# Attention's last blocks, token routing and the first expert weights, in another order

## The chip, the cores and the metric

One core of a Trainium2 chip runs the whole program in one launch. The metric is the device time in microseconds (us); of the kernel before there are three timed runs. About 0.2% (1.15 us) is what a measurement of this kernel can tell from no change.

## What is computed

Three layers follow each other, on 4 sequences of 576 tokens with 8 heads of 64 (512 columns):

```python
scores = q @ k.T / 8;  ret = scores * gamma[h] ** (s - t) for s >= t, else 0;  x = ret @ v
logits = x @ w_gate;  local = sigmoid(x @ w_local)
e[s] = argmax(logits[s]) if s == 0 or local[s] < 0.5 else e[s - 1]
x[s] = softmax(logits[s])[e] * (relu(x[s] @ w1[e]) @ w2[e])          # 8 experts, 512 -> 1024 -> 512
h = relu(x @ w_in);  u, v = halves of h;  v = (v - mean) / std
out = (u * (w_spatial @ v + b_spatial)) @ w_out
```

The expert of a token can be that of the token before it, so routing needs a scan along each sequence. All of it is computed in float32 (large products as three products of split operands).

## The kernel before, in words

**Attention** works on 18 blocks of 128 tokens. Blocks 0 to 15 are chunk c = j // 4 of sequence b = j % 4; blocks 16 and 17 (the *late* blocks) each hold the last 64 tokens of two sequences. For each block there are: `scores` (16 products k by q into the PSUM tiles sc0 and sc1, multiplied on DVE by a decay table into pm, or into ST for a late block, L299), `scaled` (POOL makes qh and kt, or a part of ST, L312 to L320), `state_update` (16 products kt by v into st, added on DVE to the running state Sbd; after a sequence's fourth chunk also into MV, which the late blocks read), `outputs` (products of Sbd by qh and of v by pm into oT, copied by ACT as xT, L366; for a late block MV by ST, L353) and `rows` (products of xT with an identity beside the gate's weights into tx, L379: that turns the block and gives its logits L, which DVE reduces, L387, and ACT copies the rows to xb, L391).

**Routing** runs for each chunk of four blocks (routing 0 to 3) and for the two late blocks (routing 4). It is a generator, advanced one step at a time between the blocks' work: the best expert of each token and a mask (L411 to L439); two small products `ap` that put tokens along the row (L444), an ACT copy uaT, two DVE scans Fc (the expert carried on, and its count); `op` (L456) gives counts of other sequences, `offs` and GF the place of each token; `pp` (L475) brings the places back to the tokens, pos_i (L478); then POOL scatters the rows of x to their place in x_sorted, one indirect DMA for each block (L480). The last step updates the tables cum, D and Pk (L491 to L505).

After routing 4 the experts are ordered by their number of tokens: key, rank, RR; gidx (which rows the experts' blocks hold), permi (which expert comes when). permi is read into a register of SP for the load of the first expert weight (`load_w(0)`, L879), and POOL gathers the first expert's two blocks with gidx (L843). `tables` computes cnt (blocks beyond the capacity; all engines read it and branch, `overflow`), the expert's starts Sr and Sri, the rows for the way back yidx, and permi2, which the loads of weights 1 to 3 use. Then PE transposes the gathered blocks (L857), ACT and DVE split them (xH L858, xL L859) and the weights (wH L888, wL L889, for each 512 KB tile), and the expert's products run (L901 to L903). The weights have four staging buffers and are split two tiles ahead.

**What sets the order.** In the attention loop the order of PE's instructions is the program's; DVE, ACT, POOL and SP are ordered by the tile scheduler. Each block's loads are issued two blocks ahead into five buffers; the late blocks are loaded in the same way, in iterations 14 and 15. PSUM tiles have one buffer each (sc0, sc1, oT, st, tx), two for routing's. After routing 4 the scheduler orders all engines, up to the section with the first weights, where PE, SP, DVE and ACT follow the program. `keep_warm` puts products of zeros on PE (L202): 14 at the start, TAIL_WARM between the steps of routing 4, WARM[1] = 34 behind the tables.

The change touches `load_blk`, `views`, `scores`, `scaled`, `outputs`, `rows`, `routing`, the loop over the blocks and what follows it up to gidx, `tables`, and the place of `load_w(1)` to `load_w(3)`.

Of the kernel before, what the change touches and what calls it, by code (L numbers as in the profile page):

```python
# [20 lines left out]
D = H * DH  # L21
# [3 lines left out]
P = 128  # L25
# [6 lines left out]
WARM = (14, 34, 2, 4)  # L32
# [120 lines left out]
def fused(tc, blk, wgl, w1, w2, wv, wu, ws, wo, bs, cst, out, dbg=None, stop=9, caps=CAPS):  # L153
# [3 lines left out]
    with top:  # L157
# [19 lines left out]
        iotap = cp.tile([P, 9], F32, name="iotap")[:, :1]  # L177
# [4 lines left out]
        ctab = cp.tile([P, 5, 8], F32, name="ctab")  # L182
# [22 lines left out]
        with ExitStack() as ph1:  # L205
# [10 lines left out]
            def load_blk(j, parts=(0, 1)):  # L216
                if j not in btiles:
                    btiles[j] = bp.tile([P, BLKW], F32, name=f"blk{j}", tag="blk")
                t = btiles[j]
                for p_ in parts:  # L220
                    lo, hi = ((0, 1024), (1024, BLKW))[p_]
                    if j >= 16 and p_ == 1:
                        for hf in range(2):
                            sl = slice(hf * 64, hf * 64 + 64)
                            SP.dma_start(out=MV[j - 16][hf][sl].rearrange("p h c -> p (h c)"), in_=blk[j, sl, 1536:])
                        hi = 1536
                    SP.dma_start(out=t[:, lo:hi], in_=blk[j, :, lo:hi])

# [3 lines left out]
            MV = [[c1.tile([P, H, DH], F32, name=f"mv{i}_{hf}") for hf in range(2)] for i in range(2)]  # L232

# [17 lines left out]

            identB = c1.tile([P, P], BF16, name="identB")
            jB = c1.tile([P, 64], BF16, name="jB")

            def small_constants():
# [4 lines left out]
                V.tensor_copy(iotap, cs("iota_p"))  # L260

# [14 lines left out]
            def views(j):  # L276
                t = btiles.pop(j)
                c, b = (j // 4, j % 4) if j < 16 else (4, None)
# [26 lines left out]
            def scaled(j):  # L305
                d = blks[j]
                if j >= 16:
                    d["ST"] = [wk.tile([P, H, 64], F32, name=f"ST{hf}", tag=("qh", "ST1")[hf]) for hf in range(2)]
                    tab = cs("q4").rearrange("p (h t) -> p h t", h=H)
                    for hf in range(2):  # L310
                        sl = slice(64 - hf * 64, P - hf * 64)
                        G.tensor_tensor(d["ST"][hf][sl], d["kk"][sl], tab[sl], op=ALU.mult)  # L312
                    return
# [7 lines left out]
                d["kt"] = kt  # L321

# [46 lines left out]
            def rows(j):  # L369
                xT = blks[j]["xT"]  # L370
                if j == 17:
                    tx = [psc.tile([P, 512], F32, name=f"tx{g}", tag=("sc1", "st")[g]) for g in range(2)]
                else:
                    tx2 = pso.tile([P, 2, 512], F32, name="tx")
                    tx = [tx2[:, g] for g in range(2)]
                for pr in range(4):
# [4 lines left out]
                if j == 17:  # L381
# [4 lines left out]
                else:  # L386
                    V.tensor_reduce(L[:, j, :], tx2[:, :, :2 * TW].rearrange("p g (h c) -> p c g h", h=2)[:, P:],  # L387
                                    axis=AX.XY, op=ALU.add)
                xb = xp.tile([P, D], F32, name="xb")
# [7 lines left out]
            zero8 = c1.tile([P, 8], F32, name="zero8")  # L397
            G.memset(zero8, 0.0)
            tabs = dict(cum=[zero8], D=[])
            kio = cs("iota_pb")[:, None, :].to_broadcast([P, 8, 4])  # L400

            def routing(c):
# [7 lines left out]
                m = wk.tile([P, nb, 1], F32, name="m", tag="rm")  # L410
                V.tensor_reduce(m, Lg, axis=AX.X, op=ALU.max)  # L411
                r = wk.tile([P, nb, 1], F32, name="r", tag="rr")
                V.tensor_scalar(r, Ls[:, :, 8:9], GATE_TH, None, op0=ALU.is_lt)
                if c == 0:
                    V.tensor_scalar(r, r, cs("first"), None, op0=ALU.max)
                er = wk.tile([P, nb, 8], F32, name="er", tag="rer")
# [3 lines left out]
                nr_ = wk.tile([P, nb, 1], F32, name="nr_", tag="rnr")  # L420
                ua = wk.tile([P, 2, 4, 8], BF16, name="ua")
# [873 lines left out]
```

## Time and profile before

| what | us |
|---|---|
| median of three runs | 575.78 (575.36 to 575.84) |
| the profiled execution's own time | 577.63 |
| its span, first to last instruction | 575.9 |
| PE busy in the span | 550.9 (96%) |
| attention and routing, up to the first expert product | about 118 |

The span is counted from the first instruction; all times of rows are from there. PE's busy time says little of a single stage, so the stage that the change touches is read from the chain of waits, the timeline and the windows.

### The profile page before, as it was taken

What the parts mean: (1) busy time and instruction counts of PE and PEld (TensorE: products, weight loads), DVE (VectorE), ACT (ScalarE), POOL (GpSimd) and SP (SyncE); (2) the same over time, 40 slices, a digit from 0 to 9 for tenths busy, and PEclk for the clock granted to TensorE, in tenths of its full rate; (3) what the DMA queues carried; (4) which work ended last, traced back from release to release, by engine and by line L of the source; (5) the groups of instructions that cost most, each with busy time, mean ns of one, the idle gap of its engine ahead of it and who ended that gap; (6) DMA issues with size and microseconds to landing.
All of it is one profiled execution on the core that took longest, in us unless ns stands there. A gap on an engine that the chain in (4) does not pass through costs nothing.

```text
span 575.9 us, 11061 instructions
## 1 busy us (share of the span) xinstructions
PE 550.9 (96%) x4272; PEld 499.5 (87%) x4273; DVE 357.2 (62%) x757; ACT 221.8 (39%) x432; POOL 214.4 (37%) x174
## 2 busy tenths in 40 slices
PE   6989888899999999999999999999999899899997
PEld 3978877389999999999999998888888799689986
DVE  2779767755555769697975435997642845475510
ACT  1222223045444445455546533322433533463322
POOL 3565661635234535656445230332004346402000
PEclk9999999979999999999999999999999999899999
DMA  8987741586544474567465423445425554642012
GB/s 306 407 293 271 245 151 32 179 316 221 195 161 139 173 226 147 193 215 222 147 204 180 150 94 74 147 119 154 143 92 170 170 156 128 184 129 74 1 73 91
DMA packets 33864, 97.49 MB, mean 169 GB/s; under 512 B 5548, under 2 KB 5932, under 8 KB 33808
## 3 DMA queue, kind: packets, MB, share of 16 engines
q1 hardware_dynamic: 27504, 76.99, 40.4%
q0 software_dynamic: 5984, 19.24, 11.0%
q8 instruction: 34, 0.56, 0.4%
q10 hardware_dynamic: 320, 0.52, 0.3%
q14 instruction: 22, 0.18, 0.1%
HBM read 77.06 MB, written 18.89 MB: 167 GB/s over the span
## 4 chain that ended last, share of the span: by engine, by line
PE 80%; DVE 10%; issue 4%; DMA 3%; ACT 2%; SPq 0%; ACTq 0%; DVEq 0%
PE acc L901 12%; PE acc L902 12%; PE acc L903 12%; PE acc L1006 11%; PE acc L1007 11%; PE acc L1008 11%; PE tx L379 2%; PE sc L292 2%; DMA CS<-in_cst 2%; PE oT L363 2%; PE tp L857 1%; PE oT L359 1%; PE st L328 1%; DMA blk<-in_blk 1%; PE tp L1167 1%
## 5 line engine op out<-in xcount | busy, mean ns | idle before, releaser
L889 POOL TENSOR_TENSOR wL<-wst,wH 128x1024 fp32r<-128x1024 f32 x23 | 58.3, 2535 | 67.6 <-ACT wH L888 67.6
L889 DVE TENSOR_TENSOR wL<-wst,wH 128x1024 fp32r<-128x1024 f32 x41 | 54.3, 1324 | 43.3 <-ACT wH L888 40.6
L901 PE MATMUL acc<-xH,wH 128*128 128x256 f32 (+7 forms) x256 | 79.2, 309 | 0.2 <-issue 0.2
L902 PE MATMUL acc<-xL,wH 128*128 128x256 f32 (+7 forms) x256 | 79.1, 309 | 0.1
L902 PE MATMUL acc<-hL,wH 128*128 128x256 f32 (+7 forms) x256 | 78.3, 306 | 0.9 <-DVE hL L920 0.9
L901 PE MATMUL acc<-hH,wH 128*128 128x256 f32 (+7 forms) x256 | 78.9, 308 | 0.0
L903 PE MATMUL acc<-xH,wL 128*128 128x256 f32 (+7 forms) x256 | 78.7, 307 | 0.0
L903 PE MATMUL acc<-hH,wL 128*128 128x256 f32 (+7 forms) x256 | 77.5, 303 | 0.0
L888 ACT CAST wH<-wst 128x1024 fp32r<-128x1024 f32 x64 | 65.0, 1050 | 15.2 <-DMA wst<-in_w 14.9
L901 PEld LDWEIGHTS acc<-xH,wH 128*128 128x128 f32 x256 | 49.4, 193 | 0.8 <-ACT xH L858 0.7
L902 PEld LDWEIGHTS acc<-xL,wH 128*128 128x128 f32 x256 | 49.3, 193 | 0.4 <-DVE xL L859 0.4
L903 PEld LDWEIGHTS acc<-xH,wL 128*128 128x128 f32 x256 | 49.4, 193 | 0.1
L902 PEld LDWEIGHTS acc<-hL,wH 128*128 128x128 f32 x256 | 48.1, 188 | 1.4 <-DVE hL L920 1.4
L901 PEld LDWEIGHTS acc<-hH,wH 128*128 128x128 f32 x256 | 48.1, 188 | 0.2
L903 PEld LDWEIGHTS acc<-hH,wL 128*128 128x128 f32 x256 | 48.1, 188 | 0.1
L1006 PE MATMUL acc<-wsH,vH 128*128 128x288 f32 x128 | 38.2, 299 | 2.2 <-ACT ze L1118 1.7
L939 ACT COPY yT<-acc 128x256 f32 (+7 forms) x32 | 13.4, 418 | 68.5 <-PE acc L903 63.2
L919 ACT ACTIVATE hH<-acc 128x256 fp32r<-128x256 f32 (+7 forms) x64 | 26.7, 427 | 33.6 <-PE acc L903 32.8
L920 DVE SCALAR_TENSOR_TENSOR hL<-acc,hH 128x256 fp32r<-128x256 f32 (+7 forms) x64 | 29.6, 474 | 13.3 <-ACT hH L919 12.9
L1008 PE MATMUL acc<-wsH,vL 128*128 128x288 f32 x128 | 37.7, 295 | 0.0
L1007 PE MATMUL acc<-wsL,vH 128*128 128x288 f32 x128 | 37.7, 295 | 0.0
L1011 POOL DMA_INDIRECT vL<-z_v,yidx x18 | 18.3, 1016 | 44.7 <-DMA z_u<-ze 40.2
(229 smaller groups left out, 1286.2 us busy)
## 6 DMA issues: line engine op xcount, KB each, us to landing
wst<-in_w SPq DMA_DIRECT2D x64, 512.0 KB
blk<-in_blk SPq DMA_DIRECT2D x34, 512.0 KB
z_v<-ze SPq DMA_DIRECT2D x18, 257.0 KB
z_u<-ze SPq DMA_DIRECT2D x18, 256.0 KB
out<-ob SPq DMA_DIRECT2D x15, 256.0 KB
raw<-in_wv SPq DMA_DIRECT2D x4, 512.0 KB
raw<-in_wu SPq DMA_DIRECT2D x4, 512.0 KB
raw<-in_wo SPq DMA_DIRECT2D x4, 512.0 KB
```

Of the source, the lines that this page charges most:

```text
L888: A.copy(wH, st)
L889: (G if u % 8 in LPOOL and u > 1 else V).tensor_tensor(wL, st, wH.bitcast(F32), op=ALU.subtract)
L901: T.matmul(acc, lhsT=wH, rhs=xH, start=first, stop=False)
L902: T.matmul(acc, lhsT=wH, rhs=xL, start=False, stop=False)
L903: T.matmul(acc, lhsT=wL, rhs=xH, start=False, stop=last)
L919: A.activation(hH[:, :C], acc[:, :C], AF.Relu)
L920: V.scalar_tensor_tensor(hL[:, :C], acc[:, :C], 0.0, hH[:, :C].bitcast(F32), op0=ALU.max, op1=ALU.subtract)
L939: A.copy(yT[d // 3][:, d % 3, bass.ds(at, C)], acc[:, :C])
L1006: T.matmul(acc, lhsT=lH, rhs=rH, start=first, stop=False)
L1007: T.matmul(acc, lhsT=lH, rhs=rL, start=False, stop=False)
L1008: T.matmul(acc, lhsT=lL, rhs=rH, start=False, stop=last)
L1011: G.indirect_dma_start(out=t.bitcast(F32), out_offset=None, in_=src[:], in_offset=bass.IndirectOffsetOnAxis(ap=yidx[:, j:j + 1], axis=0))
```

## The change

- The late blocks get tiles of their own for q and k (QK) and for ST; they are loaded in iterations 6, 7, 10 and 11, POOL scales ST in place in iterations 9 to 12, and their scores are computed at the end of iterations 13 and 14, right ahead of the scores of blocks 14 and 15. The loop ends at block 15.
- Behind the loop PE, DVE and ACT follow one written order, down to gidx: outputs 16 come ahead of the turn of block 15, outputs 17 between the steps of routing 3. `rows` is cut into `turn`, `logits` and `keep`.
- Routing: the mask is computed first, and its product and the uaT copy come a step ahead of the other product; the scan reads the second operand from PSUM; offs is replaced by selx and a second product added into pp; the copies of nF and Cb go (ACT scales esum instead). The tables cum and D are written straight into ctab and dtb; their update has a step of its own, one step later.
- permi is computed ahead of gidx and of routing 4's last table update; `tables` computes cnt ahead of Sr.
- WARM[1] goes from 34 to 22; weights 1 to 3 are loaded behind the branch on cnt.

```diff
-WARM = (14, 34, 2, 4)
+WARM = (14, 22, 2, 4)
...
+            def load_late(i, part):
+                j = 16 + i
+                if part == 0:
+                    SP.dma_start(out=QK[i], in_=blk[j, :, :1024])
+                    return
+                for hf in range(2):
+                    own, oth = slice(hf * 64, hf * 64 + 64), slice(64 - hf * 64, P - hf * 64)
+                    SP.dma_start(out=MV[i][hf][own].rearrange("p h c -> p (h c)"), in_=blk[j, own, 1536:])
+                    SP.dma_start(out=ST[i][hf][oth].rearrange("p h c -> p (h c)"), in_=blk[j, oth, 1024:1536])
...
+            def scaled_late(i, hf):
+                tab = cs("q4").rearrange("p (h t) -> p h t", h=H)
+                sl = slice(64 - hf * 64, P - hf * 64)
+                G.tensor_tensor(ST[i][hf][sl], ST[i][hf][sl], tab[sl], op=ALU.mult)
...
-                oT = psc.tile([P, 4, P], F32, name="oT", tag="sc0" if j == 17 else "oT")
+                oT = psc.tile([P, 4, P], F32, name="oT", tag={16: "sc0", 17: "sc1"}.get(j, "oT"))
...
-                for kx in range(2):
+                uaT = wk.tile([32, P], F32, name="uaT")
+                for kx in (1, 0):
                     T.matmul(ap[:32, kx * P:kx * P + N], lhsT=ua[:, kx].rearrange("p b e -> p (b e)"), rhs=tm,
                              start=True, stop=True)
-                uaT = wk.tile([32, 2, P], F32, name="uaT")
-                A.copy(uaT[:, :, :N], ap[:32, :2 * P].rearrange("p (k n) -> p k n", k=2)[:, :, :N])
+                    if kx == 1:
+                        A.copy(uaT[:, :N], ap[:32, P:P + N])
+                        yield
...
+                esc = wk.tile([32, 16], F32, name="esc")
+                A.activation(esc, cs("esum", 32), AF.Copy, scale=cnt1)
...
+                selx = wk.tile([32, nb], F32, name="selx")
+                V.tensor_tensor(selx, selp, op[:32, :1].to_broadcast([32, nb]), op=ALU.mult)
+                yield
+                pp = bank("pp", "st")
+                T.matmul(pp[:, :nb], lhsT=lG, rhs=selp, start=True, stop=False)
+                T.matmul(pp[:, :nb], lhsT=lF, rhs=selx, start=False, stop=True)
+                V.tensor_scalar(pos_i[:, j0:j0 + nb], pp[:, :nb], 512.0 * c - 1.0, None, op0=ALU.add)
...
-            for j in range(NBLK):
-                if j + 2 < NBLK:
+            for j in range(16):
+                if j + 2 < 16:
                     load_blk(j + 2)
...
+                if j in (6, 7, 10, 11):
+                    load_late(j % 2, 1 - j // 10)
                 views(j)
                 scaled(j)
+                if 8 < j < 13:
+                    scaled_late((j - 9) // 2, (j - 9) % 2)
                 scores(j)
                 advance()
...
-                if j == 16:
-                    state_update(15)
+                if j in (13, 14):
+                    views(j + 3)
+                    scores(j + 3)
                 advance()
...
+            order = tc.manual_schedule(engines={ET.PE, ET.DVE, ET.Activation})
+            order.__enter__()
+            state_update(14)
+            outputs(15)
+            state_update(15)
+            rows(14)
+            outputs(16)
+            turn(15)
+            logits(15)
+            three, four = routing(3), routing(4)
+            next(three)
+            turn(16)
+            next(three)
+            keep(15)
+            next(three)
+            outputs(17)
+            next(three)
+            next(three)
+            logits(16)
+            keep(16)
+            rows(17)
+            next(four)
+            zt = psc.tile([P, 512], F32, name="zt", tag="sc0")
+            keep_warm(zt, TAIL_WARM[0])
+            next(four)
+            next(four)
+            next(three)
+            next(three, None)
+            keep_warm(zt, TAIL_WARM[1])
+            next(four)
+            keep_warm(zt, TAIL_WARM[2])
+            next(four)
+            next(four)
...
             tables()
-            for u in range(1, 4):
-                load_w(u)
...
             overflow(tot)
+            for u in range(1, 4):
+                load_w(u)
```

## Rows read from the trace of the kernel before

**Rows 1.** The page: busy time of each engine, its share of the span, instructions.

```profile
span 575.9 us, 11061 instructions
...
PE 550.9 (96%) x4272; PEld 499.5 (87%) x4273; DVE 357.2 (62%) x757; ACT 221.8 (39%) x432; POOL 214.4 (37%) x174
```

**Rows 2.** The chain of waits: start (us), duration, what.

```profile
94.00 0.21 DVE L L387
...
100.13 0.16 DVE pos_i L478
...
102.00 0.25 PE ap L444 x2
...
111.02 3.62 DMA xg<-x_sorted,gidx
...
118.42 0.58 PE acc L902
...
119.00 0.21 PE acc L903
```

**Rows 3.** Windows: length, busy PE, PEld, DVE, ACT, POOL; PEclk, DMA share, GB/s.

```profile
113.50:115.50 2.00, 0.29 (x2) 0.00 (x0) 1.19 (x1) 0.78 (x1) 1.63 (x2) 1.00 0.83 244
...
117.00:117.50 0.50, 0.48 (x3) 0.00 (x0) 0.50 (x1) 0.44 (x1) 0.50 (x1) 0.83 0.99 352
...
124.00:124.50 0.50, 0.50 (x5) 0.50 (x5) 0.50 (x2) 0.17 (x1) 0.00 (x0) 0.84 1.05 361
```

**Rows 4.** Groups of instructions, 0 to 110 us: busy us, mean ns | idle before.

```profile
L499 DVE TENSOR_TENSOR ge<-CS,cum 128x32 f32<-128x32 f32 x4 | 5.2, 1308 | 0.0
...
L501 DVE TENSOR_TENSOR Pk<-Pk,ge 128x32 f32<-128x32 f32 x4 | 0.8, 192 | 0.0
...
L312 POOL TENSOR_TENSOR ST<-blk,c_q 64x512 f32<-64x512 f32 x4 | 5.1, 1280 | 5.1 <-DMA blk<-in_blk 2.7 <-PE tx L379 2.3
```

**Rows 5.** Timeline, 67 to 95 us: start, us, engine, line [idle before].

```profile
67.66 1.16 PE L292 MATMUL sc<-blk 64*128 64x128 f32 x16
...
69.81 1.16 PE L379 MATMUL tx<-iw,xT 128*64 128x137 f32 x16 [0.38 <-ACT xT L366]
...
79.81 0.35 PE L475 MATMUL pp<-CS,GF 32*128 32x4 f32 x2 [1.24 <-DVE GF L461]
...
87.59 1.73 DVE L299 TENSOR_TENSOR ST<-sc,c_dtab 64x256 f32<-64x256 f32 x4 [0.19 <-PE st L328]
...
92.07 1.16 PE L379 MATMUL tx<-iw,xT 128*64 128x137 f32 x16
```

**Rows 6.** The chain of waits: one block's scores, a late block's outputs.

```profile
33.95 1.09 PE sc L292 x16
...
96.80 1.11 PE oT L353 x32
```

**Rows 7.** Windows of routing 3's first steps, routing 4's, and block 13 to 15.

```profile
94.20:95.45 1.25, 0.03 (x2) 0.03 (x2) 1.12 (x8) 1.14 (x3) 0.00 (x0) 1.00 0.00 0
...
100.44:101.98 1.54, 1.49 (x7) 0.60 (x7) 1.54 (x16) 0.00 (x0) 0.90 (x1) 1.00 0.00 0
...
67.66:93.23 25.57, 22.46 (x385) 20.57 (x386) 18.65 (x55) 6.24 (x16) 14.15 (x13) 1.00 0.42 136
```

**Rows 8.** Timeline, 99 to 123 us: scatters, routing 4's places, the third weight.

```profile
101.08 1.01 POOL L480 DMA_INDIRECT x_sorted<-xb,pos_i  x1 [9.76 <-DVE nr__1474 L433]
...
104.76 0.16 DVE L478 CAST pos_i<-pp 128x2 int32<-128x2 f32 x1
...
106.19 0.96 POOL L480 DMA_INDIRECT x_sorted<-xb,pos_i  x1 [0.30 <-DVE key L561]
...
122.05 1.05 ACT L888 CAST wH<-wst 128x1024 fp32r<-128x1024 f32 x1 [3.11 <-DMA wst<-in_w]
```

**Rows 9.** Timeline of SP's queue, 113 to 114 us: the second weight.

```profile
113.72 0.30 SPq L879 DMA_DIRECT2D wst<-in_w  x1
```

**Rows 10.** DMA queues, 113 to 114 us: packets, MB, share.

```profile
q0 software_dynamic: 58, 0.21, 56.6%
```

More of the change, by code (lines that the diff above doesn't have):

```diff
@@ L181, in fused @@
         Sri = cp.tile([P, 8], I32, name="Sri")
-        ctab = cp.tile([P, 5, 8], F32, name="ctab")
+        ctab = cp.tile([P, 6, 8], F32, name="ctab")
         dtb = cp.tile([P, 5, 8], F32, name="dtb")
@@ L369, in rows, with turn @@
             def rows(j):
+                turn(j)
+                logits(j)
+                keep(j)
+            def turn(j):
                 xT = blks[j]["xT"]
-                if j == 17:
-                    tx = [psc.tile([P, 512], F32, name=f"tx{g}", tag=("sc1", "st")[g]) for g in range(2)]
+                if j == 16:
+                    tx = [psc.tile([P, 512], F32, name=f"tx{g}", tag=("oT", "st")[g]) for g in range(2)]
                 else:
@@ L415, in routing @@
                     V.tensor_scalar(r, r, cs("first"), None, op0=ALU.max)
+                if not last:
+                    V.tensor_scalar(ua[:, 1], r.to_broadcast([P, 4, 8]), -1.0, 1.0, op0=ALU.mult, op1=ALU.add)
+                else:
+                    nr_ = wk.tile([P, nb, 1], F32, name="nr_", tag="rnr")
+                    V.tensor_scalar(nr_, r, -1.0, 1.0, op0=ALU.mult, op1=ALU.add)
+                    for x in range(nb):
+                        V.tensor_scalar(uv[:, 1, x], hm, nr_[:, x], None, op0=ALU.mult)
+                m = wk.tile([P, nb, 1], F32, name="m", tag="rm")
+                V.tensor_reduce(m, Lg, axis=AX.X, op=ALU.max)
                 er = wk.tile([P, nb, 8], F32, name="er", tag="rer")
@@ L440, in routing, with bank @@
                 yield
-                ap = psr.tile([P, 512], F32, name="ap", tag="rt")
+                def bank(name, tag):
+                    return psc.tile([P, 512], F32, name=name, tag=tag) if last else \
+                        psr.tile([P, 512], F32, name=name, tag="rt")
+                ap = bank("ap", "sc1")
                 tm = jB if last else identB
-                for kx in range(2):
+                uaT = wk.tile([32, P], F32, name="uaT")
+                for kx in (1, 0):
                     T.matmul(ap[:32, kx * P:kx * P + N], lhsT=ua[:, kx].rearrange("p b e -> p (b e)"), rhs=tm,
@@ L568, in fused @@
                             op=ALU.is_equal)
+            t1 = tb.tile([P, 8, 8], F32, name="t1")
+            V.tensor_tensor(t1, RR, ie[:, None, :].to_broadcast([P, 8, 8]), op=ALU.mult)
+            V.tensor_reduce(permf, t1, axis=AX.X, op=ALU.add)
+            V.tensor_copy(permi, permf)
+            next(four)
             V.tensor_scalar(Pk, Pk, float(B * S - 1), None, op0=ALU.min)
```

163 lines of the change are left out of this document (62 added, 101 removed).

## The prediction

> **What bounds the kernel now.** I first read the totals: TensorE (PE) is busy for 96% of a span of 575.9 us [rows 1], so from the first expert on the time is matmul work, and what the change can move is the time at which that work starts. The profiled execution took 577.63 us, 1.85 above the median of 575.78; sums are made on its trace, and the difference goes onto the median. Next the chain of waits from the last attention block to the first expert product [rows 2]: logits of block 15 at 94.00, places of routing 3 (L478) at 100.13, then the gather of the first expert's tokens, 3.62 us from 111.02 to its landing, and the expert product at 118.42. The reader is to see that no matmul throughput bounds this stretch: it is a chain logits, routing, scatter, gather. Last the granted clock by stretch [rows 3]: PE is nearly idle from 113.5 to 115.5, the clock falls to its lower level (1.2 GHz) within 117.0 to 117.5 and is back at 2.4 in 124.0 to 124.5. The first 6 us of expert work run at half speed, so a microsecond of delay there can cost as little as half a microsecond.
>
> **1. The loop up to block 12.** Table updates of routings 0 and 1 (L491 to L505) move one step later, behind the next block's score products, and the DVE copies into ctab and dtb, of nF and of Cb go. On the engine, nothing gets faster where PE is the bound; what can be won is PE waiting for a late DVE or ACT. L499 has a mean of 1308 ns for 32 elements a row, against 192 for L501, the same size [rows 4]; DVE falls behind, and in the second of these places tx of block 11 waits 0.38 us for xT [rows 5]. One such wait per routing, 2 x 0.38, goes: -0.75. Against it, four POOL products of 1.28 us (L312) move from blocks 16 and 17 into iterations 9 to 12 [rows 4], where POOL also issues scatters; the nearest bounds are 0 (they fit where POOL waits for blocks) and +1.28 (one stands ahead of a qh that PE wants). I take 0, since qh is made one block ahead. Loads for the late blocks stand in SP's queue at iterations 6 to 11 in place of 14 and 15; the bytes are the same, and blocks are loaded two ahead, so 0, at most +1. Step 1: -0.75, bounds -1.5 and +1.3.
>
> The Trainium skill, SBUF — State Buffer, section Who interferes with whom, says that a DVE instruction with two SBUF inputs contends with a GpSimd instruction that reads SBUF. The trace agrees: L499 has two such inputs and 1308 ns [rows 4]. By that rule alone the four POOL products would lengthen DVE's steps beside them, and the -0.75 would be nothing.
>
> **2. From scores of block 13 (67.66) to the logits of block 15.** In the kernel before, tx of block 15 starts at 92.07 and lasts 1.16, so the stretch takes 25.57 us [rows 5]; in it PE waits 1.24 for GF of routing 2 (L475) [rows 5]. The changed order has the same products for each block (scores, 16 of them, take 1.09 [rows 6]), and:
> - adds outputs of block 16, 1.11 [rows 6], now ahead of tx of block 15: +1.1.
> - puts scores 16 directly before scores 14, and 17 before 15. Both use the same two PSUM tiles, and DVE has to empty them with four products that take 1.73 in all [rows 5]. PE's queue is in order, so it waits these 1.73 less the one routing product that stands between (two ap products take 0.25 [rows 2]): 2 x 1.6 = +3.2. Behind this wait stand state, tx and outputs of the next block; nothing covers it.
> - takes away the wait for GF, as DVE and POOL carry less there: -1.2.
> - the logits of 15 no longer stand behind the ST products of block 17: they started at 94.00, 0.77 after tx ended (93.23): -0.7.
> Together +2.4. With step 1 the logits of 15 come 1.65 later, at 95.65.
>
> **3. Routing 3.** Before, 5.9 us pass from the end of these logits (94.20) to L478 at 100.13 [rows 2], because PE has tx 16, outputs 17 and tx 17 in between. New: eight DVE steps, 1.25 [rows 7], and from the ap product to the places about what routing 4 takes now, 102.00 to 104.76, 2.8 [rows 2, 8]: 4.05, with outputs 17 beside the scans. -1.9. L478 comes at 99.9, 0.25 earlier.
>
> **4. Routing 4 and the scatters.** Before, L478 of routing 4 ends at 104.92, but the first of its two scatters starts at 106.19 only: POOL issues one per 1.27 us, and the four of routing 3 begin at 101.08 [rows 8]. New: tx 17 now stands behind routing 3's pp, so its logits come some 1.2 us after 99.9, at 101.1; then eleven DVE steps 1.5 (sixteen took 1.54, some of them of routing 3 [rows 7]); then 2.55 (the 2.8 without the split uaT copy's wait); and in the fixed order routing 3's seven table steps stand before selx of routing 4. Sixteen steps in 1.54 are 0.1 each, so +0.75. Places at 105.9, end 106.05, and POOL starts about 0.8 later (100.29 to 101.08 before [rows 2, 8]): 106.85, where the queue of four, 100.85 + 5.05, is already empty. So the last two scatters, and with them the gather, come 0.65 later than before. The wait moves from POOL's queue to DVE.
>
> **5. Gather to first product.** From the last scatters to the gather and to the products nothing changes: 118.42 + 0.65. Weights 1 to 3 now wait for the branch on cnt and for permi2, which the new order of tables puts about 1 us later behind cnt. Before, SP issued the second weight at 113.72, and in the whole of 113 to 114 the gather queue alone moved bytes [rows 9, 10], the first gather landing at 114.64 [rows 2]: the weights were behind the first gather already, so taking them away saves nothing there (0; at most -0.5 for the second gather). That costs if cover goes: the third weight's cast waited 3.11 us for its DMA until 122.05 [rows 8], on an ACT that has the first hidden rows queued behind it. At half clock PE needs it only after 48 products of 0.21 us [rows 2], so 0, bounds 0 and +1.2. The warm-up products fall from 34 to 22: off the path, 0 in time; their cover for the clock is a rival below.
>
> **Sum.** +0.65 at the expert start. If the clock rises at the same place, half of it stays, +0.3; if it rises later by as much, all. I take +0.4: 576.2 on the median (578.0 on the profiled execution).
>
> **Rivals.**
> - *The bank waits are paid and nothing comes back.* Place: sc0 and sc1 between scores 16 and 14, 17 and 15. If step 1 gives 0 in place of -0.75 and the expert start carries its delay in full, 0.65 + 0.75 = +1.4: 577.2. It decides when tx of block 15 ends over 2.4 us later than 93.23. For it: DVE's 1.73 is measured and PE has nothing else to do; against: DVE loses over ten copies. 0.20.
> - *Weights late.* Place: SP behind the branch. From a second weight issued after about 115.7 (2 us late), ACT's cast holds the hidden rows and PE stops: +1.2 on top of +0.4, 577.4. 0.10.
> - *The clock.* Twelve fewer warm-up products and another place of the idle time: if the fall does not come, the 6.8 us at half speed [rows 3] are 3.4 less: 572.8; if the rise comes earlier by half of that, 574.5. Against: PE idles longer, not less. 0.12.
> - *More comes back than I count.* PE is busy for 22.5 of the 25.57 us [rows 7], so some 1.9 of waits stand there beside GF's; if 1.3 of these go too, and step 1 gives its other end (-1.5), the expert starts 1.4 earlier, 0.65 - 0.75 - 1.3: 574.4. 0.18.
> - The third part doing nothing (weights were behind the gather before) is part of my forecast.
>
> The Trainium skill, TensorE: Matmul & The Clock Gate, section What's actually happening, says that the throttled state is the default and activity releases it. The fall after the idle stretch agrees [rows 3]; by this rule fewer warm-up products make nothing better, which is why the clock rival stays small.
>
> **Numbers.** No measurable change 0.40 (own range 575.0 to 576.9; about 0.2%, 1.15 us, is what can be told from none), slower 0.30 (the first two rivals), faster 0.30 (the last two). The range leaves out the clock staying up altogether and both slow cases together: 573.4 to 578.0.
>
> **What would show it.** Right: scores 14 and 15 start about 1.7 us after scores 16 and 17 end; tx of block 15 ends near 95.6; L478's counterpart for routing 3 near 99.9 and for routing 4 near 105.9; the last scatters wait for DVE and not for POOL; second weight issued 2 us or more later without a PE wait. Wrong: scores 14 without a wait, the gather before 110.5 or after 113, a low clock over another length than 6.8 us, or a PE wait for a weight in the first expert.

## The result, and the profile of the changed kernel

The changed kernel takes 581.45 us (median of 4 runs, 581.21 to 582.34) beside 575.81 for the kernel before (4 runs, 575.36 to 577.12): a ratio of 1.0097, 95% interval 1.0078 to 1.0116. It is 5.6 us slower, outside the range of the prediction (573.4 to 578.0). Its profiled execution took 581.49, on the median; that of before lies 1.85 above its own. Ratios leave out single executions that ran over 1.5% above the fastest of their kernel; the medians in us keep them.

| | before | changed |
|---|---|---|
| span of the profiled execution | 575.9 [rows 1] | 579.7 |
| scores of block 13 start | 67.66 [rows 5] | 71.44 |
| logits of block 15 | 94.00 [rows 2] | 102.09 |
| places of routing 3 / routing 4 | 100.13 / 104.76 [rows 2, 8] | 105.94 / 112.92 |
| first gather | 111.02 [rows 2] | 118.65 |
| expert products with xL start | 118.42 [rows 2] | 126.99 |

The totals on the page of the changed kernel answer to [rows 1]:

```profile
span 579.7 us, 11039 instructions
...
PE 555.9 (96%) x4270; PEld 504.2 (87%) x4271; DVE 350.0 (60%) x736; ACT 222.9 (38%) x437; POOL 213.8 (37%) x174
```

PE is busy for 5.0 us more with two instructions fewer, so the added time is not all idleness: part of it is the same products at half the clock. Windows of the changed kernel (the columns of [rows 3], PEclk third from the end) show where:

```profile
54.00:57.00 3.00, 2.85 (x33) 2.73 (x35) 2.97 (x7) 0.06 (x1) 2.27 (x2) 0.51 0.32 105
...
88.00:91.50 3.50, 3.50 (x42) 3.48 (x43) 2.05 (x6) 0.00 (x0) 1.42 (x2) 0.52 0.05 18
...
126.20:132.20 6.00, 5.81 (x26) 5.50 (x26) 3.48 (x4) 2.49 (x4) 0.53 (x1) 0.50 1.02 372
```

Only the last of these stretches, behind the gather, exists in the kernel before ([rows 3]: 117 to 124.5, near 7 us; here it is as long). The stretches at 54 to 57 and 88 to 91.5, inside the attention loop, are new, and ahead of each of them PE had waited. A fourth stretch, 112 to 119, is new too; most of what PE does in it is warm-up products. PE's timeline from the scores of block 13 to tx of block 15 answers to [rows 5]:

```profile
71.44 1.16 PE L308 MATMUL sc<-blk 64*128 64x128 f32 x16
...
75.83 1.16 PE L308 MATMUL sc<-QK 64*128 64x128 f32 x16
...
78.15 0.46 PE L308 MATMUL sc<-blk 64*128 64x128 f32 x2 [0.99 <-PE ap L477]
...
79.08 1.13 PE L308 MATMUL sc<-blk 64*128 64x128 f32 x14 [0.48 <-DVE ST L315]
...
85.75 0.46 PE L308 MATMUL sc<-blk 64*128 64x128 f32 x2 [0.84 <-PE op L503]
...
86.69 1.13 PE L308 MATMUL sc<-blk 64*128 64x128 f32 x14 [0.48 <-DVE ST L315]
...
89.22 2.04 PE L400 MATMUL tx<-iw,xT 128*64 128x137 f32 x16
...
96.54 1.09 PE L373 MATMUL oT<-qh,Sbd 128*64 128x128 f32 x16 [1.97 <-ACT xT L380]
...
100.88 2.10 PE L400 MATMUL tx<-iw,xT 128*64 128x137 f32 x32
```

The scores of block 16 (sc<-QK) end at 76.99, those of block 14 begin at 78.15, break off and go on at 79.08, when DVE has emptied the second bank. The same comes again ahead of block 15 (85.75 and 86.69). Behind it tx takes 2.04 us, where 1.16 stands in [rows 5]. The last line holds tx of block 15 and of 16; that of 15 ends at 102.06. The stretch from 71.44 to 102.06 is 30.6 us, against 25.57 [rows 7]. As a window (the columns of [rows 7]):

```profile
71.44:102.06 30.62, 25.82 (x417) 23.77 (x418) 16.07 (x48) 6.76 (x18) 9.22 (x9) 0.94 0.20 65
```

PE is busy for 3.4 us more than in [rows 7], with the 32 products of block 16's outputs (1.1 us) and at a mean clock of 0.94 in place of 1.00, and idle for 1.7 us more.

The 3.8 us by which the scores of block 13 are late arise earlier. Timeline of POOL, DVE and PE in iterations 9 and 10:

```profile
47.67 3.99 POOL L335 TENSOR_TENSOR ST<-ST,c_q 64x512 f32<-64x512 f32 x3 [0.68 <-DMA x_sorted<-xb,pos_i]
...
50.45 1.26 DVE L452 TENSOR_TENSOR er<-CS,r 128x32 f32<-128x32 f32 x1
...
51.74 1.04 POOL L329 TENSOR_TENSOR kt<-blk,c_ktab 128x512 f32<-128x512 f32 x1
...
51.85 0.98 DVE L457 TENSOR_TENSOR w<-w,er 128x32 f32<-128x32 f32 x1
...
52.74 1.26 POOL L335 TENSOR_TENSOR ST<-ST,c_q 64x512 f32<-64x512 f32 x1
...
53.09 1.01 DVE L463 TENSOR_TENSOR ua<-CS,vr 128x32 bf16<-128x32 f32 x1
...
54.15 0.29 PE L477 MATMUL ap<-identB,ua 128*32 128x128 bf16 x1 [2.05 <-DVE ua L463]
```

Three of POOL's four moved products run back to back for 3.99 us, then a kt, then the fourth. Three DVE steps of 32 elements a row take 1.26, 0.98 and 1.01, where 0.19 is usual ([rows 4], L501): er ends with the third moved product, w with the kt, ua with the fourth. The ap product of routing 1 waits 2.05 us for ua. State update, tx and outputs stand behind it in PE's queue, and then comes the low clock of 54 to 57. The place can be told from the starts of the scores: those of block 10 come at 50.94 (51.06 in the kernel before), those of block 11 at 59.27 (55.82), and the distance stays near 3.5 to 3.8 from there on. The wait and half of the low stretch of 3.4 us are 3.75.

The chain of waits in the tail, as in [rows 2]:

```profile
102.09 0.21 DVE L L411
...
119.93 3.97 DMA xg<-x_sorted,gidx
...
126.99 0.58 PE acc L953
```

And the timeline of the steps between, DVE and POOL, as in [rows 8]:

```profile
105.94 0.16 DVE L510 TENSOR_SCALAR pos_i<-pp 128x4 int32<-128x4 f32 x1 [0.55 <-PE pp L509]
...
107.04 0.20 DVE L411 TENSOR_REDUCE L<-tx 128x9 f32<-128x36 f32 x1 [0.56 <-PE tx L400]
...
112.11 0.14 DVE L505 TENSOR_TENSOR selx<-CS,op 32x2 f32<-32x2 f32 x1
...
112.92 0.16 DVE L510 TENSOR_SCALAR pos_i<-pp 128x2 int32<-128x2 f32 x1 [0.68 <-PE pp L509]
...
113.82 1.01 POOL L512 DMA_INDIRECT x_sorted<-xb,pos_i  x1 [2.21 <-issue]
...
115.13 0.96 POOL L512 DMA_INDIRECT x_sorted<-xb,pos_i  x1 [0.30 <-issue]
...
118.65 0.98 POOL L894 DMA_INDIRECT xg<-x_sorted,gidx  x1 [2.55 <-DVE t L661]
```

From the logits of block 15 to the places of routing 3 pass 3.85 us (6.13 before). The last two scatters now wait for these places (POOL idle 2.21; the first of them starts 0.74 behind the end of pos_i, as 0.79 in the kernel before), and the gather comes 3.52 us behind the last, as before (107.45 to 111.02, 3.57). The whole expert part is then moved by the same amount: the transposes at the start of an expert, and a product of the stage behind the experts, in the changed kernel

```profile
322.91 0.80 PE L908 MATMUL tp<-identR,xg 128*128 128x128 f32 x8
...
459.12 0.40 PE L1057 MATMUL acc<-wsH,vH 128*128 128x288 f32 x1 [0.56 <-ACT ze L1169]
```

and in the kernel before, with a window behind them:

```profile
314.48 0.80 PE L857 MATMUL tp<-identR,xg 128*128 128x128 f32 x8
...
452.51 0.40 PE L1006 MATMUL acc<-wsH,vH 128*128 128x288 f32 x1 [1.73 <-ACT ze L1118]
...
496.00:500.00 4.00, 4.00 (x11) 2.78 (x10) 0.38 (x3) 1.44 (x4) 0.99 (x2) 0.57 0.60 165
```

The distance is 8.4 at the transposes. Behind the experts the kernel before waits 1.73 for ACT where the changed kernel waits 0.56, and from 496 to 500 this one execution of before ran at 0.57 of the clock, which the changed kernel's does not. These two are 2.9 of the 4.6 us by which the distance shrinks to the end; the spans differ by 3.8 us. The medians differ by 5.6, the profiled execution of before being 1.85 above its own.

### The profile page after: what moved, and what is told of

The parts are those of the page before. It is cut to its first block, busy times and chain, and to the rows that moved or that the text cites. A ratio compares the mean times of both kernels' runs of the same rounds, so it can differ in the third digit from the quotient of the medians.

```text
span 579.7 us, 11039 instructions
## 1 busy us (share of the span) xinstructions
PE 555.9 (96%) x4270; PEld 504.2 (87%) x4271; DVE 350.0 (60%) x736; ACT 222.9 (38%) x437; POOL 213.8 (37%) x174
## 3 DMA queue, kind: packets, MB, share of 16 engines
q1 hardware_dynamic: 27536, 76.99, 39.9%
## 4 chain that ended last, share of the span: by engine, by line
PE 85%; DVE 8%; issue 2%; ACT 2%; DMA 2%; SPq 0%; POOLq 0%; ACTq 0%; DVEq 0%
PE acc L952 12%; PE acc L953 12%; PE acc L954 11%; PE acc L1059 11%; PE acc L1057 11%; PE acc L1058 11%; PE sc L308 3%; PE tx L400 3%; PE oT L377 2%; PE st L342 2%; PE oT L373 1%; PE tp L908 1%; DMA blk<-in_blk 1%; PE tp L1218 1%; DMA xg<-x_sorted,gidx 1%
## 5 line engine op out<-in xcount | busy, mean ns | idle before, releaser
L318 DVE TENSOR_TENSOR pm<-sc,c_dtab 128x512 f32<-128x512 f32 x32 | 20.6, 685 | 23.3 <-PE sc L308 20.1
```

The source lines that it names most:

```text
L318: V.tensor_tensor(pm, sc[hh], tab[:, hh], op=ALU.mult)
```

## The experiments

Theory A: the waits of PE for the two score banks, and the low clock behind them. Theory B: POOL's four products in iterations 9 to 12, which hold DVE and POOL's own queue up. Theory C: the end (order of tables, weights behind the branch, 22 warm-up products). The runs were made on four chips; on three of them the kernel before takes 565 us, on one 577. Times are compared only with runs of before on the same chip, ratios with their 95% intervals.

**The scores moved within the iteration.**

```diff
                     rows(j - 2)
+                if j in (13, 14):
+                    views(j + 3)
+                    scores(j + 3)
...
                     outputs(j - 1)
-                if j in (13, 14):
-                    views(j + 3)
-                    scores(j + 3)
```

> The changed kernel (581.4 us), with the scores of blocks 16 and 17 issued between the rows and the outputs of iterations 13 and 14 (so behind state update and rows, ahead of outputs) in place of directly ahead of the scores of blocks 14 and 15. Theory A (the two waits for the score banks, near 2.0 us each, and the low clock of 87.3 to 91.9 us behind the second): the waits fall to under 0.6 each, the stretch from scores 13 to the end of tx of block 15 falls from 30.6 to about 26.5, and the time to 577 to 578. Theory B (the POOL products of iterations 9 to 12 carry the loss): the stretch falls, but scores 13 still start near 71.4, and the time stays over 579.5. Theory C (the end: order of tables, weights behind the branch, fewer warm-up products): 581.

570.32 us, before 565.35: 1.0100 [1.0071, 1.0129]. On this chip the changed kernel itself has 1.0159 (next run), so some 0.6% came back, as much as theory A expected. But the stretch from the scores of 13 to the logits of 15 is 29.9 us (63.90 to 93.79) where 26.5 was expected, against 32.3 in the next run. Timeline of DVE and PE:

```profile
67.40 3.58 DVE L439 TENSOR_SCALAR r<-L 128x4 f32<-128x4 f32 x1
...
71.25 0.23 PE L477 MATMUL ap<-identB,ua 128*32 128x128 bf16 x1 [1.63 <-DVE ua L443]
```

A DVE step of 4 elements a row took 3.58 us, and the early ap product, which needs the step behind it, waited in front of the scores of 14. The second bank wait went, the first stayed, and the clock was low from 72 to 80: part of theory A, and a first sight of theory B's mechanism.

**The products emitted later.**

```diff
-                if 8 < j < 13:
-                    scaled_late((j - 9) // 2, (j - 9) % 2)
+                if j in (14, 15):
+                    scaled_late(j - 14, 0)
+                    scaled_late(j - 14, 1)
```

> The changed kernel with POOL's four products of the late blocks moved from iterations 9 to 12 to iterations 14 and 15 (two in each, behind that block's own products). Theory B: the wait of the second ap product of routing 1 (2.05 us at 54.15) and the low clock of 54 to 57.3 go, scores 13 start near 68 in place of 71.44, and the time falls by 3 to 3.5, to 578. Theory A: 581, since what stands behind scores 13 is the loss, or slower, because the products then run beside DVE's ST products. Theory C: 581.

574.37: 1.0159 [1.0132, 1.0187]. It tested nothing: POOL's order is not written out in the loop, the products are placed where their inputs are ready, and the order of instructions on PE, DVE, ACT, POOL and SP came out as in the changed kernel. It stands here as a measurement of that kernel on this chip.

**The tables of routing 3 behind selx of routing 4.**

```diff
-            next(three)
-            next(three, None)
             keep_warm(zt, TAIL_WARM[1])
             next(four)
+            next(three)
+            next(three, None)
             keep_warm(zt, TAIL_WARM[2])
```

> The changed kernel with the table steps of routing 3 moved behind selx of routing 4. selx came at 112.11 although its product was done near 111.1. My theory of the end: places of routing 4 come 0.7 to 0.8 earlier against the logits of block 17, and so do the scatters and the gather: 580.7. If gather and expert start hang on the tables (cnt, gidx) and not on the scatters: 581.4, or up to 0.5 more.

572.17: 1.0138 [1.0102, 1.0174], not told apart from 1.0159. From the logits of block 17 to the places of routing 4 it took 6.09 (101.27 to 107.36), against 6.18 in the run before: the gain of 0.7 was not there. It appears in the pair further down (6.18 to 5.23).

**Weights and warm-up as before.**

```diff
-WARM = (14, 22, 2, 4)
+WARM = (14, 34, 2, 4)
...
             tables()
+            for u in range(1, 4):
+                load_w(u)
...
             overflow(tot)
-            for u in range(1, 4):
-                load_w(u)
```

> The changed kernel with weights 1 to 3 issued ahead of the branch again and 34 warm-up products: the third part of the change undone. My theory: no more than 0.5 either way (580.9 to 581.9), since the second weight's transfer was behind the first gather in the kernel before as well. Theory C (weights late, or a clock that lacks the warm-up): 1 us or more faster, 580.4 or less, with the first transposes or the clock's rise earlier. If the weights now collide with the gathers: slower, and the landing of the second gather is later than 123.9.

574.52: 1.0167 [1.0131, 1.0203], against 1.0159: nothing came back, theory C has no support in this part.

**The changed kernel again, and the scores behind the loop**, on a chip where before takes 576.91:

```diff
-                if j in (13, 14):
-                    views(j + 3)
-                    scores(j + 3)
...
+            views(16)
+            scores(16)
             state_update(14)
             outputs(15)
+            views(17)
+            scores(17)
             state_update(15)
```

> The changed kernel once more, unaltered, timed on the same chip as the other runs of this call, since the first four experiments ran on a chip on which the kernel before takes 565.4 us: every theory expects a ratio to the kernel before near 1.010 (1.008 to 1.016); above 1.013 the loss depends on the chip, as it would if it hangs on which POOL product happens to stand beside a DVE step of the routing.

> The changed kernel with the scores of blocks 16 and 17 taken out of iterations 13 and 14 and issued after the loop: 16 ahead of the state update of block 14, 17 behind the outputs of block 15. Work and tables are the same; every score bank now has 0.7 to 2 us of other products between its two uses. Theory A (bank waits and the low clock behind them): PE no longer waits ahead of scores 14 and 15, the stretch from scores 13 to the end of tx of block 15 falls from 30.6 to 26 or 27, and the ratio falls by 0.6 to 0.9% against the changed kernel in this call (about 4 us), to 1.002 to 1.006. Theory B alone: by 0.2% or less. Theory C (the end: tables, weights, warm-up): no change.

Changed kernel 582.85: 1.0102 [1.0054, 1.0150]. Scores behind the loop 577.40: 1.0012 [0.9975, 1.0049]; 0.9% came back, what theory A expected, though POOL's four products were where they had been. PE's timeline of the latter, the ap product of routing 1 and the scores of blocks 14 and 15:

```profile
54.61 0.23 PE L477 MATMUL ap<-identB,ua 128*32 128x128 bf16 x1 [2.03 <-DVE ua L463]
...
75.64 1.16 PE L308 MATMUL sc<-blk 64*128 64x128 f32 x16
...
80.34 1.16 PE L308 MATMUL sc<-blk 64*128 64x128 f32 x16
```

Both scores start without a wait. The stretch from the scores of 13 to the logits of 15 is 27.3 us (70.39 to 97.67), against 30.6 in the changed kernel on this chip (74.71 to 105.28; this execution, 586.59, is the slowest of its six). But the scores of 13 start 4.3 earlier as well, ahead of anything that the edit changes: there the ap product waits 2.03 in one and 2.24 in the other, and in the changed kernel the clock is down behind it (window):

```profile
54.00:60.00 6.00, 5.55 (x59) 5.43 (x61) 4.10 (x9) 0.95 (x3) 3.15 (x4) 0.50 0.58 207
```

So on this chip the profiled pair does not separate A from B; the medians say that the place of the scores has most of the loss. The kernel before was traced here as well, once (577.49 us). One table update (L499) takes 0.97 us there, and by the profile nothing waits for it: such a step has its cost ahead of ap, not in the table updates.

**The same with tables behind selx and the two ap products together.**

```diff
                 uaT = wk.tile([32, P], F32, name="uaT")
+                if c < 3:
+                    yield
                 for kx in (1, 0):
...
                     if kx == 1:
                         A.copy(uaT[:, :N], ap[:32, P:P + N])
-                        yield
+                        if c >= 3:
+                            yield
```

> As the run before, with two more edits: the table steps of routing 3 behind selx of routing 4, and in routings 0 to 2 the product of ua's second half put back beside the first, one score block later, where PE has other work while DVE is late. Theory A with B: the early product's waits (1.13 at 29.45; 1.6 in iteration 13 of the first four experiments) go, another 1 to 2 us, and 0.7 for the tables: a ratio of 0.998 to 1.003. If the product only waits at its later place: as the run before less 0.7 us.

579.68: 1.0053 [1.0021, 1.0085]; slower than the run before where both variants of the expectation had it faster or equal. The wait at 29 fell (0.54), but near 55 it grew, and the clock went down with it (timeline, window):

```profile
55.63 0.29 PE L479 MATMUL ap<-identB,ua 128*32 128x128 bf16 x1 [3.29 <-DVE ua L463]
...
55.00:61.00 6.00, 5.37 (x57) 5.26 (x59) 4.28 (x9) 0.95 (x3) 1.97 (x3) 0.50 0.63 227
```

That is theory B's wait, one DVE step (w, 2.25 us) longer. While it is there, an edit ahead of it can cost more than it is worth.

**The products held back by their table.** q4 is loaded into q3's tile, so load and products come behind block 15; the second run has the scores behind the loop too, the third also the two edits of the run before.

```diff
-                if j in (2, 5, 8, 9):
-                    load_c({2: "q1", 5: "q2", 9: "q3", 8: "q4"}[j])
+                if j in (2, 5, 8):
+                    load_c({2: "q1", 5: "q2", 8: "q3"}[j])
...
                 scaled(j)
-                if 8 < j < 13:
-                    scaled_late((j - 9) // 2, (j - 9) % 2)
+                if j == 15:
+                    load_c("q4")
+                    for n in range(4):
+                        scaled_late(n // 2, n % 2)
...
+            CB["q4"] = CB["q3"]
```

> The changed kernel with POOL's four products of the late blocks held back alone: their table q4 is loaded into q3's tile, so its load and the products come behind the products of block 15 (POOL runs them near 80 to 86 us in place of 48 to 54). The scores of 16 and 17 stay in iterations 13 and 14. Theory B: the wait of the second ap product of routing 1 (2.0 to 2.2 us near 54) and the low clock behind it go, scores 13 start about 3 us earlier, the ratio falls from 1.010 to 1.004 to 1.006; the score-bank waits ahead of scores 14 and 15 stay at about 1.5 to 2 each. Theory A alone: 1.009 to 1.011. If the chip is one on which the wait near 54 does not occur, both expect no change, and the start of scores 13 says so.

> Both: the scores of 16 and 17 behind the loop (as in the run with ratio 1.0012) and the four products held back. If the two losses are separate and add up: 3 us less than that run, 0.995 to 0.997, faster than the kernel before. If only the bank waits count: 1.000 to 1.002.

> As the run before, with the early ap product of routings 0 to 2 beside the other one and the table steps of routing 3 behind selx of routing 4. With the ap wait near 54 gone these two should give what they were worth alone: 0.7 us for the tables and 0.5 to 1 us for the wait of 1.0 to 1.5 near 29, so 0.2 to 0.3% less than the run before. If it is slower than the run before, as the pair was without the products moved (1.0053 against 1.0012), then the later place of the product itself costs.

Before 565.86 on this chip, where the changed kernel was not timed. Products alone 570.34: 1.0079 [1.0056, 1.0103], between the figures of the two theories. With the scores behind the loop 565.59: 0.9997 [0.9982, 1.0012], short of the 0.995 to 0.997 that a plain sum of the two losses would give; the place of the scores is worth 4.75 us here. With all edits 564.12: 0.9966 [0.9946, 0.9986], faster than the kernel before. Between the last two the places of routing 4 come 5.23 behind the logits of 17 in place of 6.18, and the wait at 29 falls from 1.42 to 0.54.

**The third part of the change alone, in the kernel before.**

```diff
-WARM = (14, 34, 2, 4)
+WARM = (14, 22, 2, 4)
...
             tables()
-            for u in range(1, 4):
-                load_w(u)
...
             overflow(tot)
+            for u in range(1, 4):
+                load_w(u)
```

> The kernel before with the third part of the change alone: weights 1 to 3 issued behind the branch and 22 in place of 34 warm-up products. My prediction's step: nothing, 0.999 to 1.001. Theory C: over 1.002, with an ACT cast or PE waiting for the second or third weight, or a clock that falls earlier.

566.59: 1.0012 [0.9997, 1.0027]: no difference that can be told, as this step of the prediction had it. This is also the one trace of the old order on a chip of the 565 kind, and the version with all edits ran on the same chip. The first gather starts at 103.75 in the old order and at 104.04 with all edits; the first expert product (timeline of PE, the old order first) is

```profile
112.43 0.58 PE L901 MATMUL acc<-xH,wH 128*128 128x256 f32 x1
...
110.75 0.39 PE L959 MATMUL acc<-xH,wH 128*128 128x256 f32 x1 [0.23 <-ACT xH L916]
```

So the repaired order does not reach the gather sooner. It starts the experts 1.7 us sooner and at the full clock: its low stretch lies at 98 to 105, those of the old order at 98 to 102 and 108 to 115. All four traces with the products held back and the scores behind the loop have the low stretch there, near 97 to 105, and a first expert product of 0.38 to 0.39.

**Shares, on one chip** (before 565.05). Four runs: the changed kernel; with the products held back; with that, ap and tables but the scores in their place; with all edits.

> The changed kernel, unaltered, for the other runs of this call to be compared with on one chip: ratio 1.010 to 1.016.

> The changed kernel with the four POOL products held back behind block 15, once more, now beside the changed kernel itself. Theory B has a share of its own: 0.4 to 0.8% less than the changed kernel of this call, with scores 13 starting 1 to 4 us earlier or the DVE step r of routing 2 short where it was 3.6 us. Theory A alone: within 0.2% of it.

> Products held back, ap products together, tables behind selx, but the scores of 16 and 17 still in iterations 13 and 14. Against the next run it differs in nothing but the place of these scores: theory A gives 0.6 to 0.9% (two waits of 1.5 to 2 us and the low clock behind them), so 1.003 to 1.006; theory B alone gives the next run's ratio.

> The version that was 0.9966 of the kernel before, on this chip: 0.994 to 0.999 if it is faster than both kernels in general; 1.000 or more if that was the one chip's.

| | us | ratio to before |
|---|---|---|
| changed kernel | 574.00 | 1.0177 [1.0142, 1.0212] |
| products held back | 569.07 | 1.0089 [1.0056, 1.0123] |
| and ap, tables; scores in place | 569.34 | 1.0078 [1.0050, 1.0106] |
| and scores behind the loop | 563.68 | 0.9983 [0.9960, 1.0006] |

The products cost 4.9 us, the place of the scores 5.7, one beside the other. (With the products the load of their table, 256 KB, moves too; no run separates the two.) The ap and tables edits gave nothing in the third run. Theory B in the changed kernel, timeline of POOL, DVE and PE:

```profile
50.24 3.96 POOL L335 TENSOR_TENSOR ST<-ST,c_q 64x512 f32<-64x512 f32 x3 [3.85 <-DMA x_sorted<-xb,pos_i]
...
57.82 1.09 PE L373 MATMUL oT<-qh,Sbd 128*64 128x128 f32 x16 [0.87 <-POOL qh L326]
...
68.17 3.57 DVE L439 TENSOR_SCALAR r<-L 128x4 f32<-128x4 f32 x1
...
68.22 1.28 POOL L326 TENSOR_TENSOR qh<-blk,c_q 128x512 f32<-128x512 f32 x1
...
69.45 1.04 POOL L329 TENSOR_TENSOR kt<-blk,c_ktab 128x512 f32<-128x512 f32 x1
...
70.45 1.25 POOL L326 TENSOR_TENSOR qh<-blk,c_q 128x512 f32<-128x512 f32 x1
...
72.01 0.23 PE L477 MATMUL ap<-identB,ua 128*32 128x128 bf16 x1 [1.62 <-DVE ua L443]
...
73.69 0.46 PE L308 MATMUL sc<-blk 64*128 64x128 f32 x2 [1.45 <-issue]
```

The first product waits 3.85 us at the head of POOL's queue for the landing of routing 0's scatters (issued up to 41.90, landing 6.6 to 8.0 later), and kt and qh of the next blocks wait behind it: PE waits 0.87 for a qh at 57.82. From 50.24 to 71.70 POOL has no gap over 0.31 us, so the backlog is still there at 68 us: qh, kt, qh, and r of routing 2 takes until they are done. With the products held back the same step and the same scores are

```profile
66.99 0.17 DVE L440 TENSOR_SCALAR r<-L 128x4 f32<-128x4 f32 x1
...
70.20 0.46 PE L309 MATMUL sc<-blk 64*128 64x128 f32 x2 [0.99 <-PE ap L478]
```

The last pair isolates theory A. The scores of 13 start at 63.18 and 63.11, the logits of 15 at 93.40 and 87.73: 5.6 us for the place of the scores, as much as the medians differ (5.7). (The two profiled executions, 571.90 and 567.69, are each the slowest of its kernel here and differ by 4.2 in the end.) The window between the two (length, PE busy, PEld, DVE, ACT, POOL, PEclk, DMA share, GB/s) with the scores in place

```profile
63.18:93.40 30.22, 26.89 (x418) 24.70 (x418) 16.89 (x48) 6.67 (x16) 15.62 (x14) 0.89 0.28 92
```

and behind the loop

```profile
63.11:87.73 24.62, 23.35 (x418) 21.66 (x418) 17.44 (x48) 6.47 (x16) 15.74 (x14) 1.00 0.33 109
```

The same 418 products. PE idles 3.33 us in one and 1.27 in the other, so 2.1 of the 5.6 us are waits; the other 3.5 are the same work, 26.89 against 23.35, at a mean clock of 0.89 against 1.00. This pair does not stand alone. Read in windows of 1 us, all eleven traces with the scores of 16 and 17 in iterations 13 and 14 have a low stretch of 3.4 to 6.8 us between the scores of 13 and the logits of 15 (80 to 84 with the products held back on this chip, where no wait ahead of it is over 1 us); none of the six with these scores behind the loop has one there, nor has any trace of the kernel before.

**Once more, elsewhere.**

> The version with all three edits (scores of 16 and 17 behind the loop, products held back, ap products together and tables behind selx) a third time, 0.9966 and 0.9983 before. Faster than the kernel before in general: 0.994 to 0.999. No difference: 0.999 to 1.001.

> The changed kernel with the products held back alone, a third time (1.0079 and 1.0089, on chips where the kernel before takes 565 us). If this call's chip is one where the kernel before takes 576 us, theory B expects the wait of 2.0 to 2.2 us near 54 and its low clock to be gone there too, and 1.002 to 1.006; theory A alone 1.009 to 1.011.

All edits 564.00 against 565.54: 0.9979 [0.9958, 0.9999], the third chip on which the ratio lies below 1 (one of the three intervals reaches 1.0006). Products held back alone 569.62: 1.0072 [1.0041, 1.0103]. Again a chip of the 565 kind, so what was to be settled for the other kind is not.

## Why the prediction was wrong

**Step 1, the loop to block 12: the step that failed first.** It took the four POOL products at 0, "since qh is made one block ahead", with 1.28 as the other end, and forecast -0.75 with the loads. The scores of 13 came 3.78 late: the wait of ap, 2.05, and half of the low stretch behind it. The cover named was not there: the products run three at a time, they can stand in POOL's queue for a DMA (0.68 us at 47.67, 3.85 on another chip), and what they slow is not qh alone (0.87 at 57.82 on that chip) but the DVE steps in front of ap, which PE awaits in order. They cost 4.9 us where they were isolated, on a chip of the 565 kind. On the other kind their share is not isolated, and it is not the same in each execution: with the products in place and the scores behind the loop the wait of ap was 2.03, no low clock followed, and the time was 1.0012. The Trainium skill, SBUF — State Buffer, section Who interferes with whom, says that a DVE instruction with two SBUF inputs contends with a GpSimd instruction that reads SBUF; the prediction gave that rule the price of its own gain. The trace agrees with the rule (er 1.26, w 0.98, ua 1.01, each with two such inputs and each ending with a POOL product), and the price was too low by the wait and the clock behind it. The -0.75 itself was sound in kind: the 0.38 wait of tx of block 11 [rows 5] is gone. Not priced at all was the ap product that now stands one score block earlier; in routing 0 it waits 1.13, against 0.64 before.

**Step 2, the bank waits: right in place and size, but not in what follows.** The forecast was 1.6 each. Here the scores of 14 end at 80.21; from the end of the scores of 16 (76.99) they needed 0.23 for ap and 1.16, so 1.8 were lost; ahead of 15 (scores of 17 from 83.60 to 84.76, those of 15 ending at 87.82) it is 1.7. What failed is the price of a wait: a microsecond of PE idling was counted as one. The clock was down at 88 to 91.5, which costs about half of that stretch (1.7). The stretch grew by 5.0 where the terms gave 3.1. The 1.97 that outputs of 15 waited for xT at 96.54 are hardly the change's: ACT started this copy at 95.81, 2.6 us after its products, DVE resumed at 95.80, and such a pause stands near this place in the kernel before as well (0.31 and 1.11 at 85.92 and 87.35); with the scores in place on a chip of the 565 kind there is none. Isolated, the place of the scores cost 5.6 us, 2.1 of them waits and 3.5 the clock; by the medians it cost 5.7 and 4.75 and, on the chip of the 577 kind, 5.45.

**Step 3, routing 3: right.** 4.05 forecast from the end of the logits, 3.65 measured (102.29 to 105.94).

**Step 4, routing 4: right in kind, short by 1.** The wait did move from POOL's queue to DVE, and the gather stayed bound to the last scatter. But from the logits of 17 to the places it took 5.88 (107.04 to 112.92) where 4.8 was forecast. Most of the difference is the term of 1.5 for the eleven DVE steps, taken from a window in which sixteen steps of two routings alternate; here they follow each other and take 2.09 (107.27 to 109.36). The table steps of routing 3 ahead of selx cost near 1.0 and not 0.75, and the last products ran at half clock (the clock is down from 112 on).

**Step 5, gather and weights: right on the weights.** The weights moved alone are 1.0012. The second gather's tokens landed at 123.90 and their transposes began at 125.09, 2.3 behind the first, where 0.73 lay between the two in the kernel before (115.76 and 116.49): about 1 us more from gather to product, which the prediction had at 0. No run shows it to be the change's: over the traces this distance runs from 0.73 to 3.78, and it is 3.03 with weights and warm-up as before.

**The sum and the rivals.** 0.65 forecast at the expert start, 8.57 measured, 5.6 at the end. The rival of the bank waits had the right place and 577.2; the clock rival asked only whether the fall behind the gather would go, and no case had a fall of the clock inside the loop. The half microsecond per microsecond that the prediction granted a delay ahead of the expert part did not come: the low stretch behind the gather only moved. What the clock rival asked for, no fall behind the gather, did occur in other executions, one of the changed kernel among them (low at 115 to 122, first expert product 0.38 at 128.49).

Open is the share of the products on a chip of the first result's kind, why the clock fell behind the wait of ap in some executions and not in others, and why the two kinds of chip differ by 11 us.

## What to carry to other kernels

A product that is put where its banks are still being emptied costs PE the wait and, if the clock falls behind it, more than that again (2.1 and 3.5 us in the pair shown); look for a place where other products stand between two uses of a bank, as behind the loop here. Work moved to an engine that is "mostly idle" is priced by what stands behind it in that queue and by the steps of other engines that it lengthens while it runs (0.19 to about 1 us for a DVE step here), not by the idle share. Ask of such a step whether an engine that keeps its order waits for it. An edit of the source is not yet an edit of the order: one run here changed where the products are written and not where they run.

## What the runs showed that was not expected

- A DVE step of 4 elements a row took 3.57 us beside three POOL products without a gap, 0.17 without them. The Trainium skill, SBUF — State Buffer, section Who interferes with whom, says that tensor_scalar can enter a mode with two ports, in which the one who issues later is blocked outright. The trace fits, r being such a step and ending with POOL's last product; in which mode r ran, no run shows. It does not always wait for all of them: in the first trace of the changed kernel r took 0.44 at 49.88, beside the three moved products.
- A wait of PE of 2.0 to 2.2 us near 54 was followed by the low clock in two executions of the changed kernel (54 to 57 in the first trace, 53 to 61 in the second) and not in the run with the scores behind the loop alone.
- A product on POOL that touches no scattered data waited, by the profile, for the scatters' landing, 6.6 to 8.0 us after their issue.
- The kernel before takes 565 us on some chips and 576 on others. Its scores of 13 start at 62.64 on the first kind (the run with the weights moved alone) and at 67.66 [rows 5] and 69.26 on the other: 5.0 and 6.6 of the 11 us. Every trace from the slower kind has pauses of PE near 42 us and between 63 and 71, of up to 1.1 us each, that the profile puts down to no wait (0.99 at 64.88 in the kernel before, 1.03 at 43.77 in the changed one); the traces from the other kind have none there but at a bank wait.
